# A causal mask as a product of two triangles in PSUM instead of GpSimd's selects, and eight weight sums held back

## The chip, the core and the metric

The kernel runs on one core of a Trainium2 chip. A core has five engines that work side by side, each through its own queue in a fixed order: TensorE (products, written to PSUM), VectorE, ScalarE and GpSimd (elementwise work), and SyncE, which here starts all transfers. In the profile they are PE (with PEld for the loading of weights), DVE, ACT, POOL and SP. The metric is the device time of one execution in microseconds (us), lower is better.

## What is computed

Three layers in a row. First a linear attention with decay over 4 batches, 8 heads, 768 positions, in chunks along the sequence, with a state of 16 x 32 that is carried from chunk to chunk; then two layers over 3072 tokens with 256 features each.

```
cum = cumsum(log(clip(a, 1e-06, 1)))                  # per chunk
L = exp(cum_i - cum_j), kept where i >= j              # causal
M = (C B^T) * L
y = M x + (C state) * exp(cum)
state = exp(sum(log a)) * state + sum_j B_j x_j exp(cum_end - cum_j)
...
h = max(y w1, y w2, y w3);  x = h w_out                # 256 -> 768 -> 256
h = x w_in;  P = a0 + a1 h + a2 h^2 + a3 h^3
Q = 1 + |b0| |h| + |b1| h^2
out = (P / (Q + 1e-6)) w_out                           # 256 -> 2048 -> 256
```

The weights come as float64.

## The kernel before

**Tiling.** The sequence is cut into 6 groups of 128 positions; a group holds 128 positions of all 4 batches, T = 512 columns. Attention works on NU = 8 tiles `u` a group, each one batch and four heads, a score tile of 128x512 with the key position j on the partitions and four times 128 query positions i along the columns. The two layers behind it work on one group of 512 tokens at a time.

**One score tile in attention.** `d_mm(u)` writes cum_i - cum_j into a PSUM tile `d` (ring `pd` of two): in the first group (`u < ND`) by an fp32 product of the upper and the lower triangle with `la`, the logarithms (`tl`, made by VectorE at L477, product at L481); in the others by one bf16 product of 64 rows that holds the cumulative sums in three parts (L485). ScalarE takes the exponential into `e` (L488, ring of four), and GpSimd sets the elements with i < j to zero with an affine select (L489). `s_mm` makes two tiles C B^T at a time (L466), `m_op` multiplies `s` by `e` on VectorE (L496), `y_intra` multiplies `m` by `xn` (L507). Once a group `state` updates the carried state on TensorE (L542) and VectorE (L553, L560), `prep` makes the decay factors (L444, L447, and on GpSimd `ct` at L448), `y_inter` adds the part from the state (L518).

**Weight pieces.** TensorE uses each weight as two fp32r halves, high and low. `plan_conv` makes them from a float64 piece of 256x256: a transfer into `wraw` (ring of three, L240), then on ScalarE L245 and L248, on VectorE L246, L249 (one source) and L252 (two sources), GpSimd's sum L255, ScalarE's high half (L195 from L256), GpSimd's low half L257. There are 28 pieces: 9 of w1 to w3, 3 of wo1, 8 of win, 8 of wo2. The eight of wo2 are converted behind attention, since their buffers take attention's place.

**Sums of halves.** In the last group the second layer's output product takes wo2 as one fp32 tensor `w32`, not as halves: `w32_plan` adds high and low of eight pieces on GpSimd (L750), into buffers of the rings `wraw` and `wa`.

**What sets the order.** Every operation is given to a planner (`Plan`) with its engine, a cost in us written beside it and, for products, a due time (`when`, counted up from the costs given to `book`). `emit` plays the engines through with these costs and lets each take, of the operations that are ready, the one with the earliest latest start; the result is the fixed order of each queue. `behind` lets an operation start only after another has started. The plan has two phases: attention, and the two layers; the weight pieces belong to either.

```
def emit(self, second): ...
    i = min((i for i in wait[e] if ready[i] <= t), key=lambda i: (late[i], i))
```

Of the kernel before, what the change touches and what calls it, by code (L numbers as in the profile page):

```python
# [11 lines left out]
BF16 = mybir.dt.bfloat16  # L12
U32 = mybir.dt.uint32
AF = mybir.ActivationFunctionType
ALU = mybir.AluOpType
# [2 lines left out]

NB, NH, SEQ, HD, NS = 4, 8, 768, 32, 16
CH = 128  # L20
NG = SEQ // CH
T = NB * CH
DM, DF1, DF2 = 256, 768, 2048
# [4 lines left out]


OL = 6  # L30
ND = 8
LEAD = 3
HV, HL = "HAHP", "HHKK"
WARM = 9
# [3 lines left out]
NU = 2 * NB  # L38
F1 = DF1 // 128
F2 = DF2 // 128  # L40
# [9 lines left out]
class Plan:  # L50
# [16 lines left out]
    def op(self, engine, cost, fn, reads=(), writes=(), at=None, behind=()):  # L67
        i = len(self.ops)
        deps, after = set(), {w for t in behind for w in t.writers}
        for t in reads:  # L70
            assert (t.writers or t.given) and not t.closed
            deps.update(t.writers)
            t.readers.append(i)
        for t in writes:
            assert not t.closed
            if t.first is None:
                t.first = i
                if t.before and not t.before.given:
                    after.add(t.before.first)
                if t.prev:  # L80
                    t.prev.closed = True
                    deps.update(t.prev.writers + t.prev.readers)
            deps.update(t.writers + t.readers)
            t.writers.append(i)
        deps.discard(i)
        after.discard(i)
        self.ops.append((engine, cost, fn, [t for t in writes if t.first == i], deps, after, at,
                         self.phase))
# [67 lines left out]
def decay_attention_max_moe_rational_moe(  # L156
# [19 lines left out]
    act, dve, pool, pe = nc.scalar, nc.vector, nc.gpsimd, nc.tensor  # L176
# [89 lines left out]
    op = plan.op  # L266
# [5 lines left out]
    def mark():  # L272
        return _Tile(lambda: None)

    def load(dst, src, writes, reads=(), kb=0, nm=None):

        at = -1000.0 + FIRST.index(nm) if nm in FIRST else None
        args = ("dma", kb / 360.0, lambda: nc.sync.dma_start(
            out=dst(), in_=src() if callable(src) else src), reads, writes, at)
        if nm and nm not in FIRST:  # L280
            op(*args, behind=[cum_t])
        else:
            op(*args)
# [15 lines left out]
    when = {}  # L299
    clock = [6.0]  # L300
    wt = {}
# [9 lines left out]
    sp = at.enter_context(tc.tile_pool(name="sp", bufs=1))  # L311
# [3 lines left out]
        pools[nm] = at.enter_context(tc.tile_pool(name=nm, bufs=bufs, space=PS))  # L315

    tri_s = sp.tile([128, 2, 128], F32, name="tri_s")

    lr = [sp.tile([64, NU * CH + T], BF16, name=f"lr{i}") for i in range(2)]
    ld = [t[:, 0:NU * CH].rearrange("p (u j) -> p u j", u=NU) for t in lr]  # L320
    rd = [t[:, NU * CH:] for t in lr]
# [7 lines left out]

    cz = [sp.tile([128, 4, T], F32, name=f"cz{i}") for i in range(2)]  # L330
    cz_t, lr_t = [[mark() for _ in range(4)] for _ in range(2)], [mark() for _ in range(2)]
    (act_t, tri_t, own_t, la_t, wrev_t, cs_t, sel_t, cum_t, co_t) = (mark() for _ in range(9))
    rd_t, ld_t, re_t = ([mark() for _ in range(2)], [[mark() for _ in range(3)] for _ in range(2)],
                        [[mark() for _ in range(3)] for _ in range(2)])

# [22 lines left out]
    for i in range(2):  # L358
        for f in range(2):
            e = "dve" if f else "pool"  # L360
# [6 lines left out]
    def warm():  # L367
        for _ in range(WARM):
            pe.matmul(zp.t, zero[:, 0:CH], zero, start=True, stop=True)
    op("pe", 0.43 * WARM, warm, [zero_t], [zp], 0.0)  # L370
    load(lambda: la, aT, [la_t], kb=100, nm="a")
    load(lambda: tri_s, tri, [tri_t], kb=131, nm="t")
    op("act", 1.28, lambda: act.preload_act_table_set("natural_log"), [], [act_t])
    op("dve", 0.17, lambda: dve.tensor_scalar(out=la, in0=la, scalar1=1e-6, scalar2=1.0,
                                              op0=ALU.max, op1=ALU.min), [], [la_t])
# [23 lines left out]
    for p in range(3):  # L399
        src = pcv if p == 0 else (lambda p=p: cr(p - 1))  # L400
        op("act", 0.3, lambda p=p, src=src: copy(act, cs[:, p], src()), [pc if p == 0 else cr_t], [cs_t])
        if p < 2:
            op("dve", 0.34, lambda p=p, src=src: dve.tensor_tensor(out=cr(p), in0=src(), in1=cs[:, p],
                                                                   op=ALU.subtract),
# [8 lines left out]
    def load_cum(g):  # L413
        q, i, j = g // 3, g % 2, g % 3
        load(lambda: rd[i][0:24], cum_d[:, q].rearrange("p (g u f) i -> p g u (f i)", u=NU, g=3)[:, j],
             [rd_t[i]], [cum_t, lr_t[i]], kb=25)
        for p in range(3):
            load(lambda p=p: ld[i][24 + 4 * p:28 + 4 * p],
                 cum_d[p, q].rearrange("(g u f) j -> g f u j", u=NU, g=3)[j], [ld_t[i][p]], [cum_t, lr_t[i]], kb=16)
        for p in range(3):  # L420
            load(lambda p=p: re[i][8 * p:8 * p + 8].rearrange("h (b i) -> h b i", b=NB),
                 cum_d[p, q].rearrange("(g b h) i -> g h b i", b=NB, g=3)[j], [re_t[i][p]], [cum_t], kb=16)
# [10 lines left out]
    def book(key, cost):  # L433
        when[key] = clock[0]
        clock[0] += cost

    e0, e_t, m_t, s_t, y_t, st = {}, {}, {}, {}, {}, {}
# [33 lines left out]
    def d_mm(u):  # L471
        g, k = divmod(u, NU)
        t = new("pd", "d", 2)
        if u < ND:

            tl = new("s2", "tl", 2)
            op("dve", 0.78, lambda: dve.tensor_tensor(  # L477
                out=tl.t.rearrange("t (f i) -> t f i", f=4), in0=tri_s[:, 0:1, :].to_broadcast([128, 4, CH]),
                in1=la[:, 4 * u:4 * u + 4, None].to_broadcast([128, 4, CH]), op=ALU.mult), [tri_t, la_t], [tl])
            book(("d", u), 0.86)  # L480
            op("pe", 0.86, lambda: pe.matmul(t.t, tri_s[:, 1, :], tl.t, start=True, stop=True),  # L481
               [tri_t, tl], [t], when["d", u])
        else:
            book(("d", u), 0.22)
            op("pe", 0.22, lambda: pe.matmul(t.t, ld[g % 2][:, k], rd[g % 2], start=True, stop=True),  # L485
               [lr_t[g % 2], rd_t[g % 2], *ld_t[g % 2]], [t], when["d", u])
        e_t[u] = e = new("s4", "e", 4)
        op("act", 0.59, lambda: act.activation(out=e.t, in_=t.t, func=AF.Exp), [t], [e])  # L488
        op("pool", 0.75, lambda: pool.affine_select(out=e.t, in_=e.t, pattern=[[0, 4], [1, CH]],  # L489
                                                    compare_op=ALU.is_ge, fill=0.0, base=0,  # L490
                                                    channel_multiplier=-1), [], [e])

    def m_op(u):
        m_t[u] = m = new("s5", "m", 5)
# [86 lines left out]
        load_s(g)  # L581
        load_v(g)
    prep(0)
    for g in range(1 if ND == NU else 0, 2):
        load_cum(g)
    for s in range(NS_ALL + LEAD + 3):
        if s < NS_ALL:
            d_mm(s)
# [110 lines left out]
            psplit(of(st), hi, lo, "dve")  # L699
            xk[g].append((hi, lo))  # L700

    yk = {}

    def gy_plan(g):
        hk = []
        for f in range(F1):
            xa = new("mp2", "xa", 2)
            for e, nm in enumerate(("w1", "w2", "w3")):
                t = gy_bank(g)

                def mm(t=t, nm=nm, f=f):
                    for k in range(KD):
                        hi, lo = xk[g][k]
                        mm3(t.t, nm, k, 128 * f, (hi.t, lo.t), k == 0, k == KD - 1)
                op("pe", 6 * MM, mm, [x for p in xk[g] for x in p] + [wt[nm, 0, 256 * (f // 2)]], [t],
                   when["g", g, f, e])
                if e == 0:
                    op("act", 0.48, lambda t=t, xa=xa: copy(act, xa.t, t.t), [t], [xa])
                else:
                    op("dve", 0.61, lambda t=t, xa=xa: dve.tensor_tensor(out=xa.t, in0=xa.t, in1=t.t, op=ALU.max),  # L720
                       [t], [xa])
            hi, lo = new("hp", "hhi", F1, dtype=F32R), new("hp", "hlo", F1, dtype=F32R)
            psplit(of(xa), hi, lo, "pool")
            hk.append((hi, lo))
        yk[g] = []
        for m in range(KD):
            t = gy_bank(g)
            for f in range(F1):
                def mm(t=t, m=m, f=f):
                    hi, lo = hk[f]  # L730
                    mm3(t.t, "wo1", f, 128 * m, (hi.t, lo.t), f == 0, f == F1 - 1)
                op("pe", 3 * MM, mm, [*hk[f], wt["wo1", f // 2 * 2, 0]], [t], when["y", g, m, f])
            hi, lo = new("mp2", f"yhi{m}", 2, dtype=F32R), new("mp2", f"ylo{m}", 2, dtype=F32R)
            psplit(of(t), hi, lo, "dve", 0.48, 0.67)
            yk[g].append((hi, lo))
# [5 lines left out]
    def w32_plan(i):  # L741

        if i < 3:
            st = plan.tile("wraw", 3, lambda: cvr.tile([128, 2, 2, DM], F32, tag="wraw", name="w32"))
        else:
            st = plan.tile("wa", 2, lambda: cva.tile([128, 1, 2, DM], F32, tag="wa", name="w32"))
        for j in range(2 if i < 3 else 1):
            k = 2 * i + j if i < 3 else i + 3
            w32[k] = st, j
            op("pool", 1.23, lambda k=k, j=j: pool.tensor_tensor(  # L750
                out=st.t[:, j], in0=wsb["wo2", k][0].bitcast(F32), in1=wsb["wo2", k][1].bitcast(F32), op=ALU.add),
               [wt["wo2", 2 * k, 0]], [st], when["h", (NG - 1) * F2] - 60.0)

    def h_plan(s, c0=0, n=T):
        g, k = divmod(s, F2)
# [199 lines left out]
```

## Time and profile before

| | us |
|---|---|
| median of 3 runs (603.86 to 606.4) | 604.42 |
| the profiled execution | 604.48 |
| its span, first to last instruction | 602.6 |
| attention: up to the first product of the two layers | 125.5 |
| the six groups of the two layers | 477.1 |

The page of the profile gives for the whole span TensorE 93% busy, VectorE 88, ScalarE 73, GpSimd 77. These are averages over stages that differ, so the rows below take the program in stretches. A busy matmul row is not TensorE at its peak: matmuls are pipelined, and what one costs is read from start to start. The trace gives the granted clock of TensorE, as a share of full speed, for each stretch; attention is the only part where it is not 1.00 (0.86 on average). An engine's idle time is put down to what ended it; what an engine waits for inside an instruction, as VectorE and GpSimd can, is part of the instruction's duration.

### The profile page before, as it was taken

How to read it: one execution, taken by the hardware profiler on the slowest of the kernel's cores; microseconds unless marked ns; L12 is line 12 of the kernel's file. 1: busy time of each engine (PE TensorE's matmuls, PEld its weight loads, DVE VectorE, ACT ScalarE, POOL GpSimd, SP SyncE). 2: the span in 40 equal slices, each digit the busy share in tenths (PEclk: the TensorE clock that was granted, in tenths of full speed). 3: DMA queues.
4: the chain of work that ended last, by engine and by line, in shares of the span. 5: the costliest groups of instructions: out<-in, count | busy, mean ns of one | idle time of the engine just before them, and what ended most of it. 6: DMA issues, size and time to landing. Idle time of an engine off the chain costs nothing.

```text
span 602.6 us, 8061 instructions
## 1 busy us (share of the span) xinstructions
PE 558.5 (93%) x2710; PEld 409.2 (68%) x2710; DVE 529.5 (88%) x773; ACT 439.7 (73%) x756; POOL 465.9 (77%) x402
## 2 busy tenths in 40 slices
PE   7777676899989999999999999999999999999997
PEld 2232232367767888888888888888888888887653
DVE  6999988749979999899888998889988899888996
ACT  5666566536567887787777878778687887878883
POOL 3888898928899997787857778577786778769983
PEclk9987789799999999999999999999999999999999
DMA  7866567153300010000100001000000000000000
GB/s 233 242 211 208 180 189 214 36 176 108 102 0 1 1 36 1 1 35 2 35 1 1 35 2 35 2 0 36 0 2 0 2 35 1 1 1 17 19 1 35
DMA packets 19044, 33.70 MB, mean 56 GB/s; under 512 B 3523, under 2 KB 4027, under 8 KB 19003
## 3 DMA queue, kind: packets, MB, share of 16 engines
q1 hardware_dynamic: 19003, 33.20, 17.5%
q8 instruction: 21, 0.34, 0.2%
q14 instruction: 20, 0.16, 0.1%
HBM read 27.27 MB, written 5.91 MB: 55 GB/s over the span
## 4 chain that ended last, share of the span: by engine, by line
PE 65%; DVE 13%; POOL 7%; issue 5%; DMA 5%; ACT 2%; SPq 1%; DVEq 0%; ACTq 0%; POOLq 0%
PE pg L638 9%; PE pg L640 9%; PE pg L639 9%; PE ph L638 6%; PE ph L640 6%; PE ph L639 6%; PE po L638 5%; PE po L640 5%; PE po L639 5%; PE s L466 2%; DVE wa L246 2%; DVE wa L249 2%; DVE m L496 1%; DMA wraw<-in_w_dram 1%; PE y L507 1%
## 5 line engine op out<-in xcount | busy, mean ns | idle before, releaser
L840 POOL TENSOR_TENSOR glo<-w,ghi 128x512 fp32r<-128x512 f32 x80 | 104.8, 1309 | 16.0 <-ACT ghi L195 15.7
L638 PE MATMUL pg<-xhi,w_hi 128*128 128x512 f32 x202 | 79.2, 392 | 4.7 <-DVE xa L720 4.1
L640 PE MATMUL pg<-xhi,w_lo 128*128 128x512 f32 x202 | 78.6, 389 | 0.0
L639 PE MATMUL pg<-xlo,w_hi 128*128 128x512 f32 x202 | 78.6, 389 | 0.0
L290 POOL TENSOR_TENSOR hlo<-xa,hhi 128x512 fp32r<-128x512 f32 x36 | 50.0, 1389 | 30.7 <-ACT hhi L195 30.7
L827 ACT ACTIVATE pr<-v,qc 128x512 f32<-128x512 f32 x83 | 57.5, 692 | 18.7 <-POOL v L806 11.7
L195 ACT ACTIVATE ghi<-w 128x512 fp32r<-128x512 f32 x80 | 50.5, 632 | 24.5 <-PE po L640 22.3
L638 PE MATMUL ph<-yhi,win_hi 128*128 128x512 f32 x160 | 62.6, 391 | 2.0 <-DVE w L825 1.4
L639 PE MATMUL ph<-ylo,win_hi 128*128 128x512 f32 x160 | 62.4, 390 | 0.3 <-DVE ylo L290 0.3
L640 PE MATMUL ph<-yhi,win_lo 128*128 128x512 f32 x160 | 62.3, 389 | 0.0
L639 PE MATMUL po<-glo,wo_hi 128*128 128x512 f32 x160 | 62.3, 389 | 0.0
L638 PE MATMUL po<-ghi,wo_hi 128*128 128x512 f32 x160 | 62.2, 389 | 0.0
L640 PE MATMUL po<-ghi,wo_lo 128*128 128x512 f32 x160 | 62.2, 389 | 0.0
L832 DVE SCALAR_TENSOR_TENSOR pr<-w,co,pr 128x512 f32<-128x512 f32 x83 | 62.0, 747 | 0.0
L829 DVE SCALAR_TENSOR_TENSOR v<-v,pr 128x512 f32<-128x512 f32 x83 | 56.3, 678 | 3.6 <-ACT pr L828 3.5
L806 POOL TENSOR_TENSOR v<-t,v 128x512 f32<-128x512 f32 x44 | 57.1, 1298 | 3.0
L834 DVE SCALAR_TENSOR_TENSOR w<-v,pr 128x512 f32<-128x512 f32 x83 | 56.3, 679 | 0.6
L255 POOL TENSOR_TENSOR wa<-wa,we 128x512 uint32<-128x512 uint32 x28 | 37.0, 1321 | 24.7 <-DVE wa L252 22.8
L720 DVE TENSOR_TENSOR xa<-xa,pg 128x512 f32<-128x512 f32 x67 | 45.5, 679 | 7.1 <-ACT xa L195 5.4
L828 ACT ACTIVATE pr<-pr 128x512 f32<-128x512 f32 x86 | 50.4, 586 | 1.1
L488 ACT ACTIVATE e<-d 128x512 f32<-128x512 f32 x48 | 28.2, 594 | 28.1 <-DVE m L496 17.6
L638 PEld LDWEIGHTS pg<-xhi,w_hi 128*128 128x128 f32 x202 | 37.9, 188 | 14.4 <-DVE xa L720 5.4
(163 smaller groups left out, 1528.5 us busy)
## 6 DMA issues: line engine op xcount, KB each, us to landing
wraw<-in_wo_dram SPq DMA_DIRECT2D x11, 512.0 KB
wraw<-in_w_dram SPq DMA_DIRECT2D x9, 512.0 KB
wraw<-in_win_dram SPq DMA_DIRECT2D x8, 512.0 KB
xn<-in_xn_dram SPq DMA_DIRECT2D x6, 512.0 KB
out_dram<-ob SPq DMA_DIRECT2D x12, 256.0 KB
xt_d<-xo SPq DMA_DIRECT2D x10, 256.0 KB
xst<-xt_d SPq DMA_DIRECT2D x10, 256.0 KB
bt<-in_bz_dram SPq DMA_DIRECT2D x6, 256.0 KB
```

The source lines that it names most:

```text
L195: act.activation(out=o, in_=i, func=AF.Copy)
L290: lambda: e.tensor_tensor(out=lo.t, in0=src(), in1=hi.t.bitcast(F32), op=ALU.subtract),
L638: pe.matmul(dst, wh, hi, start=first, stop=False)
L639: pe.matmul(dst, wh, lo, start=False, stop=False)
L640: pe.matmul(dst, wl, hi, start=False, stop=last)
L806: pop(1.23, lambda: pool.tensor_tensor(out=f(v), in0=f(t1), in1=f(v), op=ALU.mult), [t1], [v])
L827: aop(0.62, lambda: act.activation(out=f(r), in_=f(v), func=AF.Ln, bias=qc), [v], [r])
L828: aop(0.48, lambda: act.activation(out=f(r), in_=f(r), func=AF.Exp, scale=-1.0), [], [r])
L829: dop(0.61, lambda: dve.scalar_tensor_tensor(out=f(v), in0=f(v), scalar=QC, in1=f(r), op0=ALU.add, op1=ALU.mult), [r], [v])
L832: dop(0.61, lambda: dve.scalar_tensor_tensor(out=f(r), in0=f(w), scalar=c(0), in1=f(r), op0=ALU.add, op1=ALU.mult), [w], [r])
L834: dop(0.61, lambda: dve.scalar_tensor_tensor(out=f(w), in0=f(v), scalar=2.0, in1=f(r), op0=ALU.subtract, op1=ALU.mult), [v, r], [w])
L840: pop(1.23, lambda: pool.tensor_tensor(out=f(lo), in0=f(w), in1=f(hi).bitcast(F32), op=ALU.subtract), [w, hi], [lo])
```

## The change

Three things. (1) The select (L489) is gone. Instead each `d` tile begins with a bf16 product of two triangles: `trib[:, 0]` is 1 where t <= j, `trib[:, 1]` is -4096 where t > i, so their product over t is -4096 x (j - i) where j > i and 0 elsewhere. The product that was there adds to it in PSUM, and the exponential makes the masked elements zero. (2) `trib` is made once by two small VectorE instructions of 128x128, from the triangles `tri_s` that are loaded anyway. (3) The sums of halves get a due time 40 us later and may only start once the first hidden tile of the last group (`hhi`) has started. The condition `u < ND` becomes `g == 0`, which is the same tiles.

```diff
+    trib = sp.tile([128, 2, 128], BF16, name="trib")
...
+    op("dve", 0.14, lambda: dve.tensor_copy(out=trib[:, 0], in_=tri_s[:, 0]), [tri_t], [trib_t])
+    op("dve", 0.14, lambda: dve.tensor_scalar(out=trib[:, 1], in0=tri_s[:, 1], scalar1=-FAR, scalar2=None,
+                                              op0=ALU.mult), [tri_t], [trib_t])
...
-        if u < ND:
+
+        def mm(w, x):
+
+            pe.matmul(t.t.rearrange("j (f i) -> j f i", f=4), trib[:, 0],
+                      trib[:, 1:2].to_broadcast([128, 4, CH]), start=True, stop=False)
+            pe.matmul(t.t, w(), x(), start=False, stop=True)
+        if g == 0:
...
-            book(("d", u), 0.86)
-            op("pe", 0.86, lambda: pe.matmul(t.t, tri_s[:, 1, :], tl.t, start=True, stop=True),
-               [tri_t, tl], [t], when["d", u])
+            book(("d", u), 1.08)
+            op("pe", 1.08, lambda: mm(lambda: tri_s[:, 1, :], lambda: tl.t), [tri_t, trib_t, tl], [t], when["d", u])
         else:
-            book(("d", u), 0.22)
-            op("pe", 0.22, lambda: pe.matmul(t.t, ld[g % 2][:, k], rd[g % 2], start=True, stop=True),
-               [lr_t[g % 2], rd_t[g % 2], *ld_t[g % 2]], [t], when["d", u])
+            book(("d", u), 0.44)
+            op("pe", 0.44, lambda: mm(lambda: ld[g % 2][:, k], lambda: rd[g % 2]),
+               [trib_t, lr_t[g % 2], rd_t[g % 2], *ld_t[g % 2]], [t], when["d", u])
         e_t[u] = e = new("s4", "e", 4)
         op("act", 0.59, lambda: act.activation(out=e.t, in_=t.t, func=AF.Exp), [t], [e])
-        op("pool", 0.75, lambda: pool.affine_select(out=e.t, in_=e.t, pattern=[[0, 4], [1, CH]],
-                                                    compare_op=ALU.is_ge, fill=0.0, base=0,
-                                                    channel_multiplier=-1), [], [e])
...
+        hk_first[0] = hk[0][0]
...
-               [wt["wo2", 2 * k, 0]], [st], when["h", (NG - 1) * F2] - 60.0)
+               [wt["wo2", 2 * k, 0]], [st], when["h", (NG - 1) * F2] - 20.0, behind=[hk_first[0]])
```

Since the costs differ, the planner draws up all queues anew. GpSimd's queue in the middle of attention, before (L255 and L257 are a weight piece's sum and low half, L489 the select, L448 `ct`):

```order
L255 TENSOR_TENSOR wa<-wa,we 128x512
L489 AFFINE_SELECT e<-e 128x512
L448 TENSOR_TENSOR ct<-ct,e_960 128x512
L257 TENSOR_TENSOR win_lo<-wa,win_hi 128x2x256
L489 AFFINE_SELECT e<-e 128x512
L255 TENSOR_TENSOR wa<-wa,we 128x512
L489 AFFINE_SELECT e<-e 128x512 x2
L257 TENSOR_TENSOR win_lo<-wa,win_hi 128x2x256
```

The same place after the change; the lines have moved by one to five (L256, L258, L453):

```order
L256 TENSOR_TENSOR wa<-wa,we 128x512
L453 TENSOR_TENSOR ct<-ct,e_1011 128x512
L258 TENSOR_TENSOR win_lo<-wa,win_hi 128x2x256
L256 TENSOR_TENSOR wa<-wa,we 128x512
L258 TENSOR_TENSOR win_lo<-wa,win_hi 128x2x256
```

What is left of GpSimd in attention is the weight pieces and one `ct` a group; the conversions keep their order, four a group, twenty in all ahead of the two layers.

TensorE's queue around one update of the state (L542), before; L485 is `d`, L444 the decay factors, L518 the part from the state:

```order
L466 MATMUL s<-cz_134,bt 128x512 x2
L542 MATMUL d<-xn,bn 64x128 x8
L507 MATMUL y<-m,xn 32x128 x4
L485 LDWEIGHTS lr_125
L485 MATMUL d<-lr_125 128x512
L444 LDWEIGHTS sel
L444 MATMUL d<-re_126,sel 128x512
L507 MATMUL y<-m,xn 32x128 x4
L518 MATMUL y<-ct,st 128x128 x8
```

The same place after the change (L549 is the state, L482 the mask, L484 `d`, L449 the decay factors, L471 `s`, L514 `y`):

```order
L549 MATMUL d<-xn,bn 64x128 x8
L482 LDWEIGHTS trib
L482 MATMUL d<-trib 128x512
L484 LDWEIGHTS lr_126
L484 MATMUL d<-lr_126 128x512
L514 MATMUL y<-m,xn 32x128 x8
L471 MATMUL s<-cz_134,bt 128x512 x2
L449 LDWEIGHTS sel
L449 MATMUL d<-re_127,sel 128x512
```

Each `d` is now two products, each with its own weights, and between the state's product and the decay factors, which need the tile that the state gives back, stand two `y` and two `s` more.

GpSimd's queue behind attention, before, with the sums of halves at L750 (L804, L806 and L824 belong to the rational functions):

```order
L255 TENSOR_TENSOR wa<-wa,we 128x512
L750 TENSOR_TENSOR w_1750<-wo_hi_1371,wo_lo_1372 128x512
L257 TENSOR_TENSOR wo_lo_1380<-wa,wo_hi_1379 128x512
L255 TENSOR_TENSOR wa<-wa,we 128x512
L804 TENSOR_SCALAR t_1785<-v,co 128x512
L750 TENSOR_TENSOR w_1789<-wo_hi_1375,wo_lo_1376 128x512
L806 TENSOR_TENSOR v<-t_1785,v 128x512
L290 TENSOR_TENSOR hlo<-xa,hhi 128x512
L824 TENSOR_TENSOR w<-w,t_1812 128x512
```

After the change they stand (L757) in the last group but one, between the low halves `hlo` and `glo` and the rational functions (L811, L813, L831):

```order
L847 TENSOR_TENSOR glo<-w,ghi 128x512
L757 TENSOR_TENSOR w_4772<-wo_hi_1368,wo_lo_1369 128x512
L291 TENSOR_TENSOR hlo<-xa,hhi 128x512
L757 TENSOR_TENSOR w_4801<-wo_hi_1372,wo_lo_1373 128x512
L831 TENSOR_TENSOR w<-w,t_4785 128x512
L847 TENSOR_TENSOR glo<-w,ghi 128x512
L811 TENSOR_SCALAR t_4828<-v,co 128x512
L757 TENSOR_TENSOR w_4840<-wo_hi_1376,wo_lo_1377 128x512
```

All eight lie among 28 GpSimd instructions in a row, and all ahead of the last group's first rational function.

## Rows read from the trace of the kernel before

**Rows 1.** The page's first line: span and instructions.

```profile
span 602.6 us, 8061 instructions
```

**Rows 2.** Busy time by stretch, PE, PEld, DVE, ACT, POOL; granted clock, DMA share, GB/s.

```profile
12.00:39.20 27.20, 20.89 (x162) 7.49 (x163) 26.22 (x37) 18.34 (x34) 21.78 (x20) 0.94 0.79 242
39.20:61.70 22.50, 15.16 (x126) 6.09 (x130) 21.38 (x30) 13.63 (x26) 18.78 (x19) 0.85 0.68 212
61.70:82.80 21.10, 13.95 (x121) 5.24 (x121) 17.72 (x26) 13.79 (x25) 17.93 (x18) 0.84 0.65 196
82.80:102.90 20.10, 14.71 (x121) 6.31 (x121) 17.37 (x26) 13.09 (x25) 18.06 (x18) 0.83 0.67 199
160.00:207.00 47.00, 43.14 (x186) 34.18 (x186) 41.82 (x59) 33.92 (x59) 44.47 (x36) 1.00 0.03 10
200.00:210.00 10.00, 10.00 (x46) 8.18 (x45) 9.99 (x16) 8.80 (x15) 10.00 (x9) 1.00 0.00 0
207.00:550.00 343.00, 343.00 (x1514) 283.73 (x1513) 309.79 (x459) 271.66 (x460) 257.63 (x212) 1.00 0.03 12
```

**Rows 3.** Groups by line up to 125.5 us: busy us, mean ns; idle before, releaser.

```profile
L489 POOL TENSOR_SCALAR_AFFINE_SELECT e<-e 128x512 f32<-128x512 f32 x48 | 38.9, 828 | 8.5 <-ACT e L488 8.5
L507 PE MATMUL y<-m,xn 128*32 128x128 f32 x384 | 22.8, 321 | 21.1 <-DVE m L496 20.3 <-PE d L485 0.7
L252 DVE SCALAR_TENSOR_TENSOR wa<-wraw,wa 128x512 uint32<-128x512 uint32 x20 | 21.9, 1097 | 0.1
L246 DVE TENSOR_SCALAR wa<-wa 128x512 f32<-128x512 f32 x20 | 15.8, 790 | 8.6 <-ACT wa L245 8.6
```

**Rows 4.** Single lines, whole run: duration ns min/median/max, first and last start.

```profile
L246 DVE TENSOR_SCALAR wa<-wa x28: 414/842/1478, 12.0 to 166.3; 128x512 f32<-128x512 f32 x28
...
L252 DVE SCALAR_TENSOR_TENSOR wa<-wraw,wa x28: 673/1126/1790, 14.3 to 168.6; 128x512 uint32<-128x512 uint32 x28
...
L255 POOL TENSOR_TENSOR wa<-wa,we x28: 1252/1273/1700, 15.9 to 170.3; 128x512 uint32<-128x512 uint32 x28
```

**Rows 5.** GpSimd and VectorE in order of time: start us, us, instruction, [idle before].

```profile
79.02 1.26 POOL L257 TENSOR_TENSOR wo_lo<-wa,wo_hi 128x512 fp32r<-128x512 f32 x1
...
79.08 1.76 DVE L252 SCALAR_TENSOR_TENSOR wa<-wraw,wa 128x512 uint32<-128x512 uint32 x1
80.76 0.68 DVE L496 TENSOR_TENSOR m<-s,e 128x512 f32<-128x512 f32 x1
...
121.22 2.39 POOL L489 TENSOR_SCALAR_AFFINE_SELECT e<-e 128x512 f32<-128x512 f32 x4
...
121.89 1.29 DVE L496 TENSOR_TENSOR m<-s,e 128x512 f32<-128x512 f32 x2 [2.51 <-POOL e L489]
```

**Rows 6.** TensorE in order of time, at either level of its clock.

```profile
63.34 1.27 PE L518 MATMUL y<-ct,st 64*128 64x128 f32 x16
...
70.48 0.66 PE L507 MATMUL y<-m,xn 128*32 128x128 f32 x8 [2.17 <-DVE m L496]
71.07 2.08 PE L466 MATMUL s<-cz,bt 64*128 64x512 f32 x4
...
90.42 0.98 PE L485 MATMUL d<-lr 64*128 64x512 bf16 x2
...
93.11 0.60 PE L485 MATMUL d<-lr 64*128 64x512 bf16 x2
...
99.42 0.43 PE L507 MATMUL y<-m,xn 128*32 128x128 f32 x8 [1.50 <-DVE m L496]
99.77 1.13 PE L466 MATMUL s<-cz,bt 64*128 64x512 f32 x4
100.83 1.09 PE L542 MATMUL d<-xn,bn 128*64 128x128 f32 x16
```

**Rows 7.** The chain of work that ended last, behind attention: start us, us, what.

```profile
162.43 1.44 POOL w L750
...
172.33 1.27 POOL w L750
...
178.63 0.50 PE ph L638
```

More of the change, by code (lines that the diff above doesn't have):

```diff
@@ L20 @@
 CH = 128
+FAR = 4096.0
 NG = SEQ // CH
@@ L30 @@
 OL = 6
-ND = 8
 LEAD = 3
@@ L331, in decay_attention_max_moe_rational_moe @@
     cz_t, lr_t = [[mark() for _ in range(4)] for _ in range(2)], [mark() for _ in range(2)]
-    (act_t, tri_t, own_t, la_t, wrev_t, cs_t, sel_t, cum_t, co_t) = (mark() for _ in range(9))
+    (act_t, tri_t, trib_t, own_t, la_t, wrev_t, cs_t, sel_t, cum_t, co_t) = (mark() for _ in range(10))
     rd_t, ld_t, re_t = ([mark() for _ in range(2)], [[mark() for _ in range(3)] for _ in range(2)],
@@ L583, in decay_attention_max_moe_rational_moe @@
     prep(0)
-    for g in range(1 if ND == NU else 0, 2):
-        load_cum(g)
+    load_cum(1)
     for s in range(NS_ALL + LEAD + 3):
@@ L700, in x_plan @@
             xk[g].append((hi, lo))
-    yk = {}
+    yk, hk_first = {}, [None]
     def gy_plan(g):
```

## The prediction

> **What bounds the kernel now.** I read the busy time by stretch first, since the change touches only the first fifth of the program and one place near its end. The profiled execution took 604.48 us, 1.9 more than its span of 602.6 [rows 1], and the median of the three runs is 604.42; so the sums below are made on 604.5. The recurrence over the sequence ends at 125.5 us; from 207 to 550 us TensorE is busy without a gap [rows 2], so nothing that GpSimd or VectorE does there sets the end unless it makes one.
>
> In the first 125.5 us no engine is full: a group of the steady part (8 score tiles, 4 weight pieces) takes 22.5, 21.1 and 20.1 us, 21.2 on average, in which TensorE is busy 14 to 15, ScalarE 13 to 14, VectorE 17 to 21, GpSimd 18 to 19 [rows 2]. What is full is something that VectorE and GpSimd share. VectorE's merge of a weight piece (L252) began at 79.08 beside a GpSimd subtraction that ran from 79.02 to 80.28, and ended at 80.84, 0.56 after it: it stood still for all of the other [rows 5]. Undisturbed it takes 0.67, on average 1.10; L246, and L249 alike, takes 0.41 undisturbed and 0.79 on average [rows 3, 4]. Products that read PSUM, as `m` (L496), don't show this. So I add up, for one group, everything that excludes the other: 8 selects at 0.60 (four in a row took 2.39 [rows 5]) = 4.8; 9 GpSimd sums, differences and products at 1.25 [rows 4] = 11.2; on VectorE 8 passes like L246 and 5 like L252, each less some 0.07 by which neighbours overlap (the `m` behind that L252 starts at 80.76, ahead of its end [rows 5]) = 8 x 0.34 + 5 x 0.60 = 5.7. That is 21.7 against 21.2 measured: this exclusion is what paces the stage. The Trainium skill (SBUF — State Buffer, section "SBUF: two separate sides") calls it an exclusive lock, held for the whole instruction, with the loser blocked; by that rule every select gives back its whole time, which is the second rival below.
>
> **The selects go.** 48 of them were busy 38.9 us, 0.83 each, of which 0.60 is their own and the rest waiting [rows 3, 5]. A group loses 4.8 and its exclusive sum falls to 16.9. That is the floor of this term; the ceiling is no gain at all, 21.2.
>
> **The masks come, on TensorE.** 48 bf16 products of 128x512 from 128 rows. No such row stands in the trace; the nearest is the bf16 product `d` (64 rows, same columns): two in a row took 0.60, 0.30 each, at the higher level of the clock, and 0.98, 0.49 each, at the lower [rows 6]. So a group gets 2.4 to 3.9 us more of TensorE. Is that hidden? At the higher level a group needs 8 x 0.35 (`y`) + 4 x 1.06 (`s`) + 9 x 0.30 (`d` and the decay product) + 1.1 (state) + 1.3 (`y` from the state) = 12.1 [rows 6], with masks 14.5. That is below 16.9, so the cover exists but is 2.4 us wide; at the granted clock of now (0.83 to 0.85) it is busy 14.6, with masks 17 to 18.5, and the cover is gone. I take 0.30: TensorE's idle time in this stage is mostly `y` waiting for `m` (21.1 us [rows 3]), a wait that the selects and the blocked VectorE make, and the clock was granted at 0.94 in the stretch 12 to 39 with its shorter waits and fell to 0.83 to 0.85 in those with 5 to 7 us of idle time a group [rows 2]; at 70.48 a wait of 2.17 is followed by `s` at 2.08 instead of 1.13 [rows 6].
>
> **Other limits at the shorter group.** ScalarE has 13 to 14 a group. A group moves about 4.2 MB (20.1 us at 199 GB/s); in 17.3 us that is 243 GB/s, what the stretch 12 to 39 ran at with the transfer engines 0.79 busy [rows 2]. So four things lie between 14 and 17 us, coupled by queues that run in a fixed order; I take a group at 17.3, just above the floor, because the present stage also runs at the sum of its exclusions. The three measured groups give back 3 x 3.9 = 11.7. In 12 to 39.2 (11 selects, 6.6 us) the transfers are nearer to their limit, so I take 3 (between 0 and 6.6). From 102.9 to 125.5, 22.6 us, four selects at the very end run alone and `m` waits 2.51 for them [rows 5]; the changed order spreads the weight pieces up to the last `m`, so I count this as one more group: 22.6 - 17.3 = 5.3 (2.4 to 6.1). Together 20.0. The two casts that make `trib` stand ahead of the first `tl` on VectorE; they are a quarter of L246's 0.41 in size, so 0.1 to 0.8 with their starts, 0.3 taken. `m` now waits for ScalarE's exponential directly, and `e` comes free a GpSimd step earlier; nothing new queues behind that. The attention stage ends near 106 instead of 125.5. What follows depends on it alone: all 20 pieces of the first five matrices are still converted ahead of it and the eight of the sixth behind it, in the same order on every queue.
>
> **The eight sums move.** They stood on GpSimd between the last conversions and the first rational functions; three lie in the chain between 162.43 and 173.6, 1.27 to 1.44 each, and the chain goes on to the product at 178.63 [rows 7]. In 160 to 207 TensorE was idle 3.9 us [rows 2], which bounds the gain; the last conversions, VectorE's backlog and the wait for the tile of group 2 stay, so I take 2.5 (0 to 3.9). Their new place is the group ahead of the last, inside 207 to 550, where GpSimd is busy 258 of 343 us, three quarters [rows 2]. They are spread over 28 of its instructions, so 20 others at some 1.2 us, 32 us at that share, get 8 x 1.3 us more: for this stretch GpSimd is full. In 200 to 210 it was busy 10.00 of 10 with sums among its work, and TensorE stayed full with its 46 products [rows 2]. So nothing, at most the 3.9 that the same sums were part of before; I take 0.3. The staging buffers that they fill are free from the last conversion on.
>
> Sum: 604.5 - 20.0 + 0.3 - 2.5 + 0.3 = 582.6.
>
> **Rivals.**
> The forecast, groups of 17 to 18.5: 577 to 588, near 582.6. Chance 0.55.
> The exclusion stays the only bound: groups of 16.5 (16.9 by the same 0.98 at which they run now), so 3 x 4.7 + 6.5 + 6.1 = 26.7, and the whole 3.9 of the sums: 604.5 - 30.6 + 0.3 = 574. For it: the match of 21.7 with 21.2. Against it: TensorE at 14.5 and the transfers leave no slack. Chance 0.12.
> TensorE takes over at half of its present idle time: busy 13.5 to 14 with a clock only partly up, masks 2.8, idle 3: 19.5 a group. That gives 3 x 1.7 + 2 + 3 = 10, and 2 for the sums: 592 (588 to 600). The Trainium skill (TensorE: Matmul & The Clock Gate, section "A second HAM failure mode: psum-queue depth-cycling") describes an engine that swings between the two levels because it pauses between groups of products, and there the work itself is not at fault; the 0.83 to 0.85 here agrees with that, and by it the products added would be paid at the lower level. Chance 0.22.
> Slower: the masks lie in TensorE's own loop `y`, `s`, `d`. If the clock stays where it is, masks cost 3.9 and a group is 14.6 + 3.9 plus idle time; it decides from 2.7 us of idle time a group on. With 4 it is 22.5, 1.3 more than now in five groups: 604.5 + 6.5 - 2 = 609. Against it: idle time is 5.4 to 7.3 now because of what is removed, and `d` to `m` gets shorter (a select and its handover out, 0.3 to 0.5 in). Chance 0.06.
> No change: the gain in attention is eaten by the transfers (the sixth matrix or a tile lands late) or the sums cost their late group what attention gave: within 3 us of 604. Chance 0.05.
>
> **How the numbers follow.** About 0.5%, 3 us, is what a measurement of this kernel can tell from no change. The first three cases are faster, 0.89; same 0.05; slower 0.06. The range runs from 573 to 595: it takes in the second case and the nearer half of the third, and leaves out some 0.1 above and less than 0.1 below.
>
> **What would show it.** Right: the last `y` product ends near 106 us; VectorE's L252 and L246 fall from 1.10 and 0.79 towards 0.9 and 0.65; the granted clock of the steady groups is above 0.9; masks take 0.3 from start to start; TensorE's idle time in the 45 us behind attention is 1 to 2 us less; TensorE has no gap where the sums now stand. Wrong: a granted clock still near 0.84 with TensorE busy over nine tenths (third or slower case); waits of ScalarE or SyncE for weight pieces that land late (the transfers); gaps of TensorE in the group ahead of the last.

## The result

The changed kernel takes 585.85 us (median of four runs, 585.03 to 586.62); the kernel before, beside it, 604.34. The ratio is 0.9688, interval 0.9661 to 0.9714: 3.1% faster. The forecast was 582.6 in a range of 573 to 595; the gain is 18.5 us where 21.9 were expected.

The page of the changed kernel, its first line, the engines' busy time, and three of the rows in 40 slices:

```profile
span 583.9 us, 8072 instructions
...
PE 562.1 (96%) x2758; PEld 412.9 (71%) x2758; DVE 525.6 (90%) x775; ACT 436.8 (75%) x756; POOL 424.5 (73%) x354
...
DVE  6999999699799989989889889989898889988996
...
POOL 2565576488778867696667777687767997869983
PEclk9998999999999999999999999999999999999999
```

The span is 18.7 us shorter than in [rows 1]. Attention ends at 108.2 instead of 125.5 and gives 17.3 of it; the layers take 475.7 instead of 477.1. Attention is the first seven and a half slices of 14.6 us. From the second to the seventh VectorE (DVE) is at nine tenths or more, and the granted clock (PEclk) sags in one slice only.

Busy time by stretch, which answers to [rows 2]: PE, PEld, DVE, ACT, POOL, then granted clock, DMA share, GB/s. The first four stretches go from one `ct` product (L453) to the next, so each is a group; the fifth holds the moved sums, and the last is the four groups together.

```profile
24.80:42.80 18.00, 16.87 (x149) 6.80 (x148) 18.00 (x27) 12.75 (x24) 10.70 (x9) 1.00 0.84 263
42.80:61.90 19.10, 16.44 (x130) 7.51 (x129) 17.80 (x28) 11.38 (x21) 9.70 (x9) 0.91 0.64 213
61.90:79.20 17.30, 15.57 (x147) 6.48 (x139) 16.82 (x27) 12.94 (x24) 10.43 (x9) 1.00 0.73 222
79.20:94.30 15.10, 14.02 (x135) 6.39 (x131) 14.95 (x23) 12.03 (x22) 10.69 (x9) 1.00 0.69 208
...
453.00:487.00 34.00, 34.00 (x151) 28.16 (x150) 28.52 (x43) 25.26 (x45) 34.00 (x29) 1.00 0.05 16
...
24.80:94.30 69.50, 62.91 (x548) 27.18 (x547) 67.58 (x102) 49.10 (x89) 41.52 (x33) 0.98 0.72 227
```

A group is 17.4 us on average (17.3 was forecast), TensorE is granted 0.91 to 1.00, and VectorE, which had 1 to 3 us to spare in a group before, has now almost none: 67.6 busy of 69.5. The groups by line up to 108.2, which answer to [rows 3] (busy us, mean ns | idle before, releaser):

```profile
L503 DVE TENSOR_TENSOR m<-s,e 128x512 f32<-128x512 f32 x48 | 31.9, 679 | 0.4 <-PE s L471 0.4
L256 POOL TENSOR_TENSOR wa<-wa,we 128x512 uint32<-128x512 uint32 x19 | 25.3, 1330 | 34.1 <-DVE wa L253 34.1
L482 PE MATMUL d<-trib 128*128 128x512 bf16 x48 | 18.8, 392 | 1.4 <-DVE st L567 1.2
L253 DVE SCALAR_TENSOR_TENSOR wa<-wraw,wa 128x512 uint32<-128x512 uint32 x20 | 18.8, 939 | 0.1
L514 PE MATMUL y<-m,xn 128*32 128x128 f32 x384 | 18.5, 287 | 6.5 <-DVE m L503 5.8 <-ACT w_hi L196 0.5
L250 DVE TENSOR_SCALAR wa<-wa 128x512 uint32<-128x512 uint32 x20 | 18.1, 904 | 0.1
L247 DVE TENSOR_SCALAR wa<-wa 128x512 f32<-128x512 f32 x20 | 16.2, 808 | 2.7 <-ACT wa L246 2.6
```

Two more rows of the kernel before, up to 125.5:

```profile
L255 POOL TENSOR_TENSOR wa<-wa,we 128x512 uint32<-128x512 uint32 x20 | 26.6, 1328 | 9.2 <-DVE wa L252 8.6 <-DMA wraw<-in_win_dram 0.6
L249 DVE TENSOR_SCALAR wa<-wa 128x512 uint32<-128x512 uint32 x20 | 14.7, 737 | 0.3
```

TensorE's idle time ahead of `y`, nearly all of it spent on `m`, fell from 21.1 to 6.5 us. But the three VectorE passes over a weight piece did not get faster as a whole: 0.94 (was 1.10), 0.90 (0.74, where the forecast took 0.79 for both short passes) and 0.81 (0.79). And GpSimd now waits 34.1 us for VectorE's L253 (8.6 for L252 before). VectorE leads.

What a mask costs, TensorE in order of time in the last steady group (start us, us):

```profile
82.89 0.39 PE L482 MATMUL d<-trib 128*128 128x512 bf16 x1
83.21 0.39 PE L484 MATMUL d<-lr 64*128 64x512 bf16 x1
83.53 0.39 PE L482 MATMUL d<-trib 128*128 128x512 bf16 x1
83.85 0.39 PE L484 MATMUL d<-lr 64*128 64x512 bf16 x1
```

Start to start it is 0.32, as `d`: 128 rows cost no more than 64.

Why VectorE's passes stay slow is seen in one place, GpSimd first and then VectorE, both in the changed kernel:

```profile
74.54 1.27 POOL L258 TENSOR_TENSOR wo_lo<-wa,wo_hi 128x512 fp32r<-128x512 f32 x1 [0.74 <-ACT wo_hi L196]
```

```profile
74.46 0.70 DVE L560 TENSOR_TENSOR d<-d,co_raw 128x512 f32<-128x512 f32 x1
75.07 1.03 DVE L250 TENSOR_SCALAR wa<-wa 128x512 uint32<-128x512 uint32 x1
76.02 1.11 DVE L567 SCALAR_TENSOR_TENSOR st<-st,e,d 128x128 f32<-128x128 f32 x4
```

L250 starts at 75.07, needs 0.34 to 0.41 undisturbed, and ends at 76.1, 0.29 after the GpSimd instruction has ended at 75.81. The weight pieces' own GpSimd work does this, and it is still all there.

### The profile page after: what moved, and what is told of

Same layout as the page of the kernel before. It is cut to its first block, busy times and chain, and to the rows that moved or that the text cites. A ratio compares the mean times of both kernels' runs of the same rounds, so it can differ in the third digit from the quotient of the medians.

```text
span 583.9 us, 8072 instructions
## 1 busy us (share of the span) xinstructions
PE 562.1 (96%) x2758; PEld 412.9 (71%) x2758; DVE 525.6 (90%) x775; ACT 436.8 (75%) x756; POOL 424.5 (73%) x354
## 3 DMA queue, kind: packets, MB, share of 16 engines
q1 hardware_dynamic: 19003, 33.20, 17.7%
## 4 chain that ended last, share of the span: by engine, by line
PE 52%; DVE 21%; POOL 14%; issue 5%; DMA 4%; ACT 2%; SPq 1%; POOLq 0%; DVEq 0%; ACTq 0%
PE pg L644 7%; PE pg L645 7%; PE pg L646 7%; PE ph L644 5%; PE ph L645 5%; PE ph L646 5%; PE po L645 5%; PE po L646 5%; PE po L644 4%; DVE wa L253 2%; POOL glo L847 2%; DVE wa L247 2%; DVE wa L250 2%; DVE m L503 2%; POOL v L813 2%
## 5 line engine op out<-in xcount | busy, mean ns | idle before, releaser
L256 POOL TENSOR_TENSOR wa<-wa,we 128x512 uint32<-128x512 uint32 x28 | 36.9, 1316 | 43.2 <-DVE wa L253 43.2
L291 POOL TENSOR_TENSOR hlo<-xa,hhi 128x512 fp32r<-128x512 f32 x36 | 50.3, 1398 | 20.2 <-ACT hhi L196 20.1
L813 POOL TENSOR_TENSOR v<-t,v 128x512 f32<-128x512 f32 x44 | 57.9, 1317 | 2.8
L646 PEld LDWEIGHTS pg<-xhi,w_lo 128*128 128x128 f32 x202 | 37.9, 188 | 7.9
```

Source lines behind the costliest of these rows:

```text
L291: lambda: e.tensor_tensor(out=lo.t, in0=src(), in1=hi.t.bitcast(F32), op=ALU.subtract),
L646: pe.matmul(dst, wl, hi, start=False, stop=last)
L813: pop(1.23, lambda: pool.tensor_tensor(out=f(v), in0=f(t1), in1=f(v), op=ALU.mult), [t1], [v])
```

## The experiments

Theory: VectorE and GpSimd exclude each other, and this paces attention; the masks are hidden on TensorE. Rivals: the selects cost as a step between the exponential and `m`; TensorE is the next bound; the sums carry more than they seem to. Each ratio is against the kernel before, run beside it on the same chip (604.4 to 605.8 us).

**Which half of the change does it.** mask_only puts the sums back at their old due time, sums_only is the kernel before with the sums held back:

```diff
-               [wt["wo2", 2 * k, 0]], [st], when["h", (NG - 1) * F2] - 20.0, behind=[hk_first[0]])
+               [wt["wo2", 2 * k, 0]], [st], when["h", (NG - 1) * F2] - 60.0)
```

> The changed kernel with the eight sums of weight halves back at their old due time, early in the two layers. Theory (the mask frees the engine that is shared, the sums add a little of their own): attention ends near 108 as in the changed kernel, the sums stand in the crowded stretch behind it again and cost 1.3 to 2.5 us, so 587 to 588.5. Rival A (the sums are worth nothing, the gain behind attention is only the new order of the queues): 585.5 to 586.5. Rival B (the sums carry more than attention): over 590.

> The kernel before with the sums of halves held back and nothing else. Theory: TensorE's idle time in the 80 us behind attention falls by 2 to 2.5 us and one to 1.2 us of it comes back late, so 602 to 603.3. Rival A: the sums only pay behind the shorter attention, then 604.3. Rival B: the late place costs more than the early one gives, then 605 or more.

mask_only: 587.26 us, ratio 0.9693 (0.9668 to 0.9719). sums_only: 604.12, ratio 0.9977 (0.9960 to 0.9995), that is 1.4 us (0.3 to 2.4). The mask is nearly all of the gain. What the sums do on top of it, 0.0005 of ratio, lies inside the intervals. The traces tell it more finely; the first 82 us of the layers in the kernel before, sums_only, mask_only and the changed kernel (columns as above):

```profile
125.50:207.50 82.00, 75.00 (x325) 59.62 (x322) 70.47 (x89) 54.21 (x94) 67.34 (x53) 1.00 0.22 71
```

```profile
124.30:206.30 82.00, 77.52 (x337) 61.79 (x334) 69.61 (x93) 56.12 (x98) 60.79 (x47) 1.00 0.21 71
```

```profile
110.00:192.00 82.00, 75.93 (x329) 60.39 (x326) 72.68 (x92) 55.37 (x96) 71.63 (x56) 1.00 0.21 71
```

```profile
108.20:190.20 82.00, 77.47 (x336) 61.67 (x333) 72.53 (x94) 56.48 (x98) 64.25 (x50) 1.00 0.21 71
```

TensorE is idle 7.0 and 6.1 with the sums early, 4.5 with them late. So they give 1.6 to 2.5 early. Over the whole of the layers (477.1, 475.6, 476.2, 475.7) only 0.5 to 1.5 is left. Of the other 1.0 to 1.1, 0.4 to 0.6 is lost again late, where the last 55 to 60 us hold 4.5 to 4.7 us of idle time with the sums late, 4.1 without; what takes the rest was not found.

**Place or load of the selects.** idle_selects lets GpSimd do 48 selects on a tile that nobody reads, beside the masks; mask_and_selects puts the old selects back on `e`, so that the mask is made twice:

```diff
+    scr = sp.tile([128, T], F32, name="scr")
...
+        op("act", 0.59, lambda: act.activation(out=e.t, in_=t.t, func=AF.Exp), [t], [e, em])
+        op("pool", 0.75, lambda: pool.affine_select(out=scr, in_=scr, pattern=[[0, 4], [1, CH]],
+                                                    compare_op=ALU.is_ge, fill=0.0, base=0,
+                                                    channel_multiplier=-1), [em], [], when["d", u] + 1.5)
```

> The changed kernel with 48 selects on GpSimd on a tile that nobody reads, started beside each exponential: GpSimd's and the shared resource's load of before, without the selects standing between the exponential and the product m. Theory (the selects cost because VectorE stands still beside them): groups of some 21 us again, attention ends at 122 to 127, 600 to 604. Rival A (the selects cost as a step between the exponential and m): 585 to 589. Rival B (half by each): 592 to 597.

> The changed kernel with the selects put back on e, so that the mask is made twice. Theory (VectorE and GpSimd's exclusion paces, TensorE has room for the masks): as the kernel before with the sums moved, 602 to 606, a group of 21 to 22. Rival (TensorE's loop was near its limit before, too, as in the slower case of the prediction): 608 to 612.

603.55 (0.9971, 0.9955 to 0.9987) and 603.98 (0.9993, 0.9965 to 1.0020). Selects that no one waits for cost as much as those that `m` waits for: nearly the whole gain of the change is gone, attention ends at 125.9 and 126.0. idle_selects by line up to there:

```profile
L502 POOL TENSOR_SCALAR_AFFINE_SELECT scr<-scr 128x512 f32<-128x512 f32 x48 | 39.3, 819 | 1.5
L509 DVE TENSOR_TENSOR m<-s,e 128x512 f32<-128x512 f32 x48 | 31.9, 677 | 4.3 <-PE y L520 4.3
L253 DVE SCALAR_TENSOR_TENSOR wa<-wraw,wa 128x512 uint32<-128x512 uint32 x20 | 25.1, 1254 | 0.2
```

`m` waits for no select, L253 takes 1.25 us (1.10 before the change), and the 20th weight piece reaches L253 at 115.2, as in the kernel before (107.7 in the changed kernel). But not all of the loss comes by VectorE. The last `m` starts at 114.6 (107.1 in the changed kernel, 124.4 before); after it TensorE waits for the last group's `ct`, which stands in GpSimd's queue behind selects and weight pieces:

```profile
122.04 2.08 PE L531 MATMUL y<-ct,st 64*128 64x128 f32 x16 [9.50 <-POOL ct L455]
```

So of the 17.7 us by which attention is longer than in the changed kernel, some 7.5 are products `m` that come later, and most of the rest is this wait for GpSimd's own full queue. The selects cost as load on GpSimd, not as a step ahead of `m`; how much of that load is paid by VectorE standing still and how much by GpSimd being full, these times alone don't separate. And with selects and masks both in the loop (mask_and_selects) it is no slower than before: TensorE had the room. One rival stays: the change and both of these kernels have newly drawn queues, and no kernel here has small selects in the old order. Against it: three orders of attention with selects (the kernel before and these two) all come to 604, while those without lie between 580 and 592.

**Are the masks hidden?** no_mask leaves out the 48 products, and with them the causal mask; the queues keep their order:

```diff
-            pe.matmul(t.t.rearrange("j (f i) -> j f i", f=4), trib[:, 0],
-                      trib[:, 1:2].to_broadcast([128, 4, CH]), start=True, stop=False)
-            pe.matmul(t.t, w(), x(), start=False, stop=True)
+            pe.matmul(t.t, w(), x(), start=True, stop=True)
```

> The changed kernel without the 48 products of triangles; the queues keep their order. The causal mask is left out, nothing takes its place. Theory (VectorE, by its own work and by what GpSimd blocks, paces the stage, and the products are hidden on TensorE): within 2 us of the changed kernel, 584 to 587. Rival (TensorE is the next bound, the products are paid): 48 times 0.3 to 0.39 is 14 to 19 us, of which more than a third comes back, 580 or less.

584.18, ratio 0.9662 (0.9610 to 0.9714): within 2 us of the changed kernel, with overlapping intervals. 48 x 0.32 = 15 us of products cost at most a few: in the profiled execution (581.43, the shortest of four; the longest is 587.53) attention ends at 105.2, 3.0 earlier. The granted clock of attention is 0.92 there and 0.98 with the masks, so what they cost is seen only net of what the clock took back.

**Taking from GpSimd what is left.** low_half_all takes the low half of each weight piece on VectorE, as the diff shows, low_half_alternate of every other one, low_half_ahead of every other one but not of wo2; low_half_no_mask is low_half_all without the masks' products; after_again is the changed kernel once more:

```diff
-        plan.op("pool", 1.3, lambda: pool.tensor_tensor(out=lo(), in0=af(), in1=hi().bitcast(F32),
-                                                        op=ALU.subtract), [a], [tok])
+        e_lo, c_lo = (dve, 0.61) if True else (pool, 1.3)
+        plan.op("dve" if e_lo is dve else "pool", c_lo, lambda: e_lo.tensor_tensor(
+            out=lo(), in0=af(), in1=hi().bitcast(F32), op=ALU.subtract), [a], [tok])
```

> The changed kernel with the low half of every weight piece of a float64 source taken on VectorE instead of GpSimd. Theory (VectorE and GpSimd exclude each other, and the sum of what they do to SBUF paces the stage): a piece then holds the shared resource for some 0.55 instead of 1.25, four pieces a group make 2.8 less, 17.4 becomes 14.6, but TensorE needs 14.5 and does not run without any idle time, so a group comes to 15.5, 5 groups give 9: 577, between 573 and 582. Rival (VectorE is full by its own work, which grows by 2.4 a group): a group of 18 to 19.5, so 589 to 597.

> The same for every other weight piece. Theory of the shared resource: half of the gain, 1.4 a group, 5 groups make 7 at most, 579 to 583. Rival (VectorE is full by its own work): 588 to 591.

> low_half_all (all low halves on VectorE) without the products of triangles; the causal mask is left out. low_half_all took 592 instead of 586 although VectorE's instructions ran nearly undisturbed there and VectorE was idle 14 us more. Theory (with VectorE relieved TensorE, masks included, became the bound there): 578 to 584, a group of some 15.5. Rival (VectorE's longer queue delays m and the engines wait for each other in turn, masks or not): 589 to 592.

> The changed kernel once more, beside the two that follow on one chip, to be compared with them in the same runs: 585 to 587.5, ratio 0.967 to 0.970.

> As low_half_alternate, but only for pieces converted ahead of the layers; the eight pieces of wo2 keep GpSimd. In low_half_alternate attention ended 1.7 us earlier than in the changed kernel, and the 45 us behind it gave one back. If that was VectorE's added work there, this one keeps the gain: 583.5 to 585, 1.5 to 2 under the changed kernel of this call. If it was only the scatter of the order: within 0.8 of it.

low_half_all 592.14 (0.9787, 0.9762 to 0.9812), low_half_alternate 585.50 (0.9683, 0.9656 to 0.9709), low_half_no_mask 590.60 (0.9762, 0.9730 to 0.9795), after_again 586.22 (0.9682, 0.9650 to 0.9714), low_half_ahead 588.65 (0.9707, 0.9681 to 0.9733). Here my theory failed: no gain that can be told from none, and with all pieces a loss of 6 us. low_half_all by line up to the end of its attention, 114.4:

```profile
L504 DVE TENSOR_TENSOR m<-s,e 128x512 f32<-128x512 f32 x48 | 31.9, 679 | 7.7 <-PE s L472 7.7
L253 DVE SCALAR_TENSOR_TENSOR wa<-wraw,wa 128x512 uint32<-128x512 uint32 x20 | 15.1, 757 | 0.0
L250 DVE TENSOR_SCALAR wa<-wa 128x512 uint32<-128x512 uint32 x20 | 10.2, 508 | 0.0
L259 DVE TENSOR_TENSOR w_lo<-wa,w_hi 128x512 fp32r<-128x512 f32 x9 | 6.5, 723 | 1.8 <-ACT w_hi L196 1.8
```

The passes run far less disturbed (0.76 and 0.51), but VectorE now stands idle 7.7 us for `s` ahead of `m`. Without the masks it is hardly better, so their products aren't the cause; the granted clock of attention fell from 0.94 to 0.85 by that, so TensorE's load as a whole is not excluded. The planner, told that VectorE does the low halves, drew all queues anew: the 20th piece reaches L253 at 98.3 instead of 107.7, while the 32nd `m` comes at 85.4 instead of 78.0. What was saved on the pieces was spent ahead, and the `m` left over run alone at the end, with VectorE half empty (columns as above):

```profile
100.00:110.00 10.00, 9.32 (x70) 2.92 (x70) 5.08 (x10) 5.56 (x10) 1.28 (x1) 0.83 0.15 54
```

That the redrawn order is the cause is argued, not shown: the same split in the old order wasn't tried. The next pair shows how much the order alone can do.

**Is it VectorE?** Both kernels take away one VectorE pass over each piece, the clamp L247. no_clamp leaves the instruction out; clamp_small, shown here, keeps it on 16 of 512 columns, so that every queue keeps its order.

```diff
-            out=af(), in0=af(), scalar1=F64_LOW, scalar2=F64_HIGH, op0=ALU.max, op1=ALU.min), [], [a])
+            out=af()[:, :, 0:8], in0=af()[:, :, 0:8], scalar1=F64_LOW, scalar2=F64_HIGH, op0=ALU.max, op1=ALU.min), [], [a])
```

> The changed kernel without one VectorE pass over each weight piece, the clamp of its absolute value (L247); the clamp is left out, which these weights don't need. It was busy 19.9 us in attention, 0.83 each, 0.34 of it its own work from start to start. Theory (VectorE by its own work and what GpSimd blocks of it paces the stage; the blocked time goes on to the next pass): 23 times 0.34 is 7.8, less what TensorE's floor takes, 578 to 582. Rival A (its whole busy time comes back): 567 to 573. Rival B (the engines wait for each other in turn, no single one paces): 584 to 587.

> The changed kernel with the clamp of each weight piece cut to 16 of its 512 columns; the rest of the clamp is left out, which these weights don't need. Without the instruction the planner had drawn new queues, VectorE then waited 20 us for TensorE, and the time rose to 589.6; here all queues keep their order, so only VectorE's work changes. Theory (VectorE's own and blocked time paces the stage): an instruction falls from 0.34 to some 0.1, 20 of them give 4.8, so 581 to 583, attention ends near 104. Rival A (the whole busy time of 0.83 comes back): 570 to 574. Rival B (VectorE's work doesn't pace, or the blocked time only moves to the next instruction and eats the gain): 585 to 587.

no_clamp 589.63 (0.9751, 0.9725 to 0.9776), slower; clamp_small 580.04 (0.9597, 0.9574 to 0.9619), 5.1 to 5.5 us faster than the changed kernel. Less work for VectorE is time, and the same saving with redrawn queues is a loss: 0.0154 of ratio, 9.3 us, lie between two kernels that do almost the same. clamp_small's attention ends at 104.8 (108.2 and 109.0 in the two profiles of the changed kernel); the layers gain 2.3 to 2.7, since the eight pieces of wo2 are converted there. The pass itself:

```profile
L250 DVE TENSOR_SCALAR wa<-wa 128x512 uint32<-128x512 uint32 x20 | 15.0, 751 | 0.1
L247 DVE TENSOR_SCALAR wa<-wa 128x16 f32<-128x16 f32 x20 | 11.1, 557 | 2.6 <-ACT wa L246 2.5
```

It has 16 columns and is still busy 0.56: nearly all of that is waiting for GpSimd. Of the 20 passes the 14 that meet a GpSimd instruction end 0.03 to 0.04 after it; the other six take 0.16 to 0.17. What went wrong in no_clamp, two of its groups by stretch and a wait of its TensorE:

```profile
27.90:49.50 21.60, 19.23 (x137) 7.75 (x133) 16.62 (x26) 13.74 (x26) 12.72 (x10) 0.84 0.82 236
49.50:70.80 21.30, 19.53 (x138) 8.28 (x137) 17.46 (x25) 13.43 (x24) 11.94 (x9) 0.76 0.69 213
```

```profile
51.26 0.59 PE L480 MATMUL d<-trib 128*128 128x512 bf16 x1 [1.39 <-ACT e L496]
51.78 0.61 PE L482 MATMUL d<-lr 64*128 64x512 bf16 x1
...
56.98 0.61 PE L480 MATMUL d<-trib 128*128 128x512 bf16 x1
57.52 0.60 PE L482 MATMUL d<-lr 64*128 64x512 bf16 x1
```

TensorE is busy nine tenths at a granted clock of 0.84 and 0.76, and a mask takes 0.52 to 0.54 from start to start. This is the prediction's third case, in a kernel that it wasn't about: groups of 21.5, with VectorE 4 to 5 us idle in each. Which of the moved instructions brought it about wasn't tried.

clamp_small leaves out a part of the computation, and none of the other kernels is faster than the changed one by more than the measurement can tell.

## Why the prediction was right, and where it was not

**What bounds.** Right in kind. idle_selects shows that the selects cost as load, not as a step, and the traces show what was full. Take every GpSimd instruction and every VectorE pass that works on SBUF, the tiles outside PSUM, alone (those of the weight pieces, `bn` and `xlo`): one or the other runs for 61.5 of the 63.7 us from 39.2 to 102.9 before, where VectorE is busy 56.5 and GpSimd 54.8; for 59.5 of 61.4 in three groups of idle_selects (42.0 to 103.4); and for 58.3 of 69.5 after the change. And in the attention of the kernel before, each of the 48 passes over a weight piece that start more than 0.1 us ahead of the end of a running GpSimd instruction ends 0.28 to 0.29 (one source) or 0.54 to 0.55 (two) after it. So the exclusion paced the stage before, and it is no longer full now; VectorE is, with 67.6 of 69.5.

An estimate of how VectorE's time in a steady group splits, with the starts of neighbours for its own work (`m`, L253 and full passes 0.60, L247 and L250 0.34, a state piece 0.26) and standing still as what is left of its busy time:

| VectorE, us a group | before, 39.2 to 102.9 | after, 24.8 to 94.3 |
|---|---|---|
| own work | 12.5 | 12.0 |
| standing still beside GpSimd | 6.4 | 4.9 |
| idle | 2.4 | 0.5 |
| together | 21.2 | 17.4 |

**The selects go.** The size was right (3.9 forecast, 3.9 measured), the way there only in part: by the table 1.5 came from less standing still, 1.9 from VectorE's idle time, which is now used up. The other 0.5 is work, and here luck helped: the three groups before held 12 passes L252, but the four after only 13 of L253, not four a group as the section on the change has it, so the groups became shorter in part because weight pieces were put off. So the sign that I had named, L252 and L246 falling to 0.9 and 0.65, did not come: 0.94 for the first, but 0.81 and 0.90 for the two short passes. I read this so that a VectorE that is never late starts its passes into GpSimd's instructions more often; no run separates that. The prediction listed four limits near 17 us, and VectorE's own 12.0 plus what GpSimd blocks was not among them; it is the one that holds. By the rule in the Trainium skill (SBUF — State Buffer, section "SBUF: two separate sides"), an exclusive lock held for the whole instruction, selects of 48 x 0.60 = 28.8 us of lock time are gone. The trace agrees that a pass stands still until the GpSimd product beside it ends, but only 17.3 us came back. I read this so that a lock costs nothing while nobody asks for it; the table agrees, since by its estimate VectorE stood still for 4.9 of GpSimd's 10.4 us a group.

**The masks.** Right: 0.32 from start to start against 0.30, hidden but for at most a few us (no_mask), and the granted clock of attention rose to 0.98, as TensorE's waits got shorter. The slower rival would have had a group of 14.6 + 3.9 and its idle time; mask_and_selects, which is that case at its hardest, was no slower than before.

**The last stretch.** This is the term that was mis-sized. I took 102.9 to 125.5 for one group and 5.3 for its gain. VectorE there, in the kernel before:

```profile
114.01 1.27 DVE L496 TENSOR_TENSOR m<-s,e 128x512 f32<-128x512 f32 x2
115.20 1.14 DVE L252 SCALAR_TENSOR_TENSOR wa<-wraw,wa 128x512 uint32<-128x512 uint32 x1
116.26 0.68 DVE L496 TENSOR_TENSOR m<-s,e 128x512 f32<-128x512 f32 x1
...
121.89 1.29 DVE L496 TENSOR_TENSOR m<-s,e 128x512 f32<-128x512 f32 x2 [2.51 <-POOL e L489]
123.77 1.29 DVE L496 TENSOR_TENSOR m<-s,e 128x512 f32<-128x512 f32 x2 [0.59 <-PE s L466]
```

Counted by products `m`, the 40th of 48 starts at 114.0, and the last eight take 10.4 us, since the pieces are over with the L252 at 115.20. After the change the 40th starts at 92.5, and the last eight take 14.6 with pieces among them (the 20th L253 starts at 107.67). So the first five groups gained 21.5 (5.0, 1.4, 5.5, 4.0, 5.6) and the last gave 4.2 back: 17.3. Part of the 21.5 is work put off: by the 40th `m` 19 pieces had come to L252 before the change, 16 to L253 after it. Spreading the pieces up to the end was no gain there, it was where part of the earlier gain is paid.

The prediction's windows, by the `m` that lie in them (the 12th is the last ahead of 39.2, the 35th the last ahead of 102.9):

| | forecast | measured |
|---|---|---|
| first stretch, less the casts for `trib` | 2.7 | 5.4 |
| three steady groups | 11.7 | 13.7 |
| last stretch | 5.3 | -1.9 |
| attention | 19.7 | 17.3 |

The last term was 7.2 too high and the other two 4.7 too low; that the errors largely cancel is luck. Of the missing 3.4 us, attention has 2.4 and the sums 0.8 (2.2 net forecast, 1.4 in the layers).

**The sums.** 2.5 early was what the trace shows (7.0 to 4.5), but 0.9 of it belongs to the new order of attention (mask_only). GpSimd is full where they now stand (34.00 of 34), and TensorE has no gap there, as forecast. Late, 0.4 to 0.6 is lost instead of 0.3. Net they are worth 1.4 alone and too little to measure behind the masks.

**The transfers** did not bind: 227 GB/s in the steady groups. The forecast's 4.2 MB a group is itself a slip, 20.1 us at 199 GB/s are 4.0; no term hung on it.

## What to carry to other kernels

Where two engines exclude each other, add up what each does and look for work that a third engine can take: it pays even if nobody waits for that work, as idle_selects shows by its loss, of which about half was one product, `ct`, caught behind it in the queue. But the gain ends where one of the two is full by its own work and the blocked time, as VectorE is here, so work out that sum too. And count progress in pieces of work, not in stretches between markers that the change itself moves. When a planner draws up the queues, an experiment that takes an instruction out should leave a tiny one in its place: the redrawn order was worth more (9.3 us) than the work removed (5).

## What was not expected of the hardware

A VectorE pass over 16 columns, 0.16 us at its shortest, was busy 0.56 on average beside GpSimd's products, and one over 512 columns 0.81: what a pass costs there is set by the neighbour more than by its size. The products `m`, which read PSUM and one tile of SBUF, took 0.68 on average in every kernel here, whatever GpSimd did.
